# Half a group later: moving the attention of groups 4 to 7 behind the sums of a seven-product MLP2, and twelve row pairs instead of eight

## The chip, the cores and the metric

The kernel runs on one core of a Trainium2 chip. The metric is device time in microseconds (us) of that core; a result is the median of several executions. A program on one core has no second die to be compared with, so an execution counts as slow when it is over 1.5% above the fastest of the same kernel; such executions are left out of the ratios.

I number groups of two row tiles as the code does, 0 to 7. "Group 3's MLP2" in the change's short description is index 2. In group k, `c, d` are the two tiles of group k+1 and `e, f` those of group k+2. Lines of the changed kernel stand three lower than those of the kernel before in the part that matters (L667 became L664, L647 became L644, L698 became L695, L397 became L394).

## The reference

One transformer block in bfloat16, 2048 rows of 576, 32 heads of 18, MLP width 4608.

```
h  = x + attention(layernorm(x), wqkv) @ wo     # each row attends to rows s, s-2, ..., s-14
h2 = h + gelu(layernorm(h) @ w1 + b1) @ w2 + b2
```

The attention is a sliding dilated window of eight: a row's logits are eight dot products per head. The kernel does that on VectorE (multiply, then add up), and gives TensorE only the projections and the MLP.

## The kernel before

Row tiles go through the MLP in groups of two. TensorE does, for each group, MLP1 (324 matmuls), the projection `wo` of the next group's attention, and MLP2. VectorE does the attention of a later group meanwhile. Two pieces of it matter here, the query-key product with its maximum, and the value sum:

```python
def att_qk_one(j, i, home):            # 2.55 us multiply + 2.87 us of adds + 0.4 us
    att_qk_a(j); halo(j, 1); att_qk_b(j, i, 0, home)

def att_pv_a(j):                       # value sum, multiplication: 2.55 us
    ... in0=v_ring[j % 2] ..., in1=probs ..., op=ALU.mult

def att_pv_b(j):                       # its adds: 2.15 + 0.46 us, result in q_all[:, j]

def pv_sum(j):                         # cut: att_pv_a, halo, att_pv_b
    ...

def halo(j, t):                        # next tile's shifted keys or values, 144 KB
    nc.sync.dma_start(out=ring[j % 2][:, j // 2, :], in_=kv_dram[j, 0:P, t - 1, :])
```

`v_ring` holds one plane that each tile has to load anew. So the value sum of the second tile must wait for a load that can only start when the first tile's multiplication has read the plane.

A finished value sum is stored (`send_o`), then read back transposed (`read_o`) as `oT`, the weights of the projection.

MLP2 of groups 2 to 7 treats `rows` of the 18 row pairs with seven matmuls instead of eight (Strassen and Winograd's scheme): VectorE forms sums of activations (`h_sums`, tiles t=0 to 3) and of weights (`w2_sums`). The order on TensorE in group 5, whose projection comes first (group 4 has the same start and end; with 12 row pairs it has no `(7, hi)` and puts `"rest"` right behind `"6"` and `"d"`):

```python
steps = ["wo", "hc", (1, all_), "b", "h", "e", (7, lo), (2, all_), (6, all_), "6", ... (7, hi), "rest",
         "in", (5, all_), "f", "exp", (4, all_), "21", "22", "o1", "4", (3, all_), "12", "o0", "3"]
```

A number is one of the seven products on TensorE. `"b"`, `"d"`, `"f"` copy a bank of PSUM, the memory in which TensorE leaves its sums, on ScalarE. `"h"`, `"6"`, `"7"`, `"exp"`, `"4"`, `"3"` are hooks where other work is put into the engines' lists; `"rest"`, `"o1"`, `"o0"` are the output adds on VectorE that free PSUM banks.

The kernel before, in the loop over groups from 2 on (cut):

```python
ROWS = {2: 8, 3: 12, 4: 12, 5: 16, 6: NM, 7: NM}
m1[0] += [c_(pv_sum, d), c_(send_o, d), c_(read_o, d)]          # second value sum: in MLP1
m1[1] += [c_(att_qk_one, f, 1, home ^ 1), c_(att_max, (e, f))]  # second query-key product and maximum: in MLP1
x["exp"] += [c_(exps, e, f), c_(att_den, e, f)]
x["4"] += [c_(att_pv_a, e), c_(halo, e, 2)]                     # first value sum: in MLP2
x["3"] += [c_(att_pv_b, e), c_(send_o, e), c_(read_o, e)]
x["7"] += [c_(att_qk_one, GROUPS[k + 3][0], 0, home)]           # first query-key product: in MLP2
```

Of the kernel before, what the change touches and what calls it, by code (L numbers as in the profile page):

```python
# [12 lines left out]
F32 = mybir.dt.float32  # L13
# [4 lines left out]
def kernel(  # L18
# [16 lines left out]
    H = 32  # L35
    Dh = D // H
    W = 8
# [18 lines left out]
    GROUPS = [ATT_ORDER[i:i + 2] for i in range(0, NT, 2)]  # L56
# [14 lines left out]
    x_all = wpool.tile([P, NT, D], BF16, name="x_all")  # L71
# [11 lines left out]
    logits = wpool.tile([P, 2, W, H], F32, name="logits")  # L83
    probs = wpool.tile([P, 2, W, H], BF16, name="probs")
# [242 lines left out]

    side = {}

    def logit_of(js):  # L330
        home, i = side[js[0]]
        return (x_all[:, 13:16:2, 0:2 * W * H].bitcast(F32).rearrange("p i (w h) -> p i w h", w=W)
                if home else logits[:])[:, i:i + len(js)]

    def sides(js):
        i = side[js[0]][1]
        return slice(i, i + len(js))

    def halo(j, t):
        if j >= 2:  # L340
# [3 lines left out]
    def att_qk_a(j):  # L344
        nc.vector.tensor_tensor(out=prod[:], in0=k_ring[j % 2], in1=q_all[:, j, :].unsqueeze(1)  # L345
                                .to_broadcast([P, W, D]), op=ALU.mult)

    def att_qk_add(j, steps):
        for o, a, c in steps:
            n = (c - a if c < 9 else 9) * H  # L350
            nc.vector.tensor_tensor(out=prod[:, :, o * H:o * H + n], in0=prod[:, :, a * H:a * H + n],  # L351
                                    in1=prod[:, :, c * H:c * H + n], op=ALU.add)

    def att_qk_b(j, i, skip=0, home=0):
        side[j] = (home, i)
        out = logit_of([j])[:, 0]
        att_qk_add(j, ((0, 0, 9), (0, 0, 4), (0, 0, 2), (0, 0, 1))[skip:])
        nc.vector.tensor_tensor(out=out, in0=prod[:, :, 0:H], in1=prod[:, :, 8 * H:9 * H], op=ALU.add)
        if j // 2 + 1 < W:
            nc.vector.memset(out[0:1, j // 2 + 1:W, :], -1e9)  # L360
# [12 lines left out]
        halo(j, 1)  # L373
        att_qk_rest(j, i)

    def att_qk_one(j, i, home):
        att_qk_a(j)
        halo(j, 1)
        att_qk_b(j, i, 0, home)

    def att_exp(*js):
        lg = logit_of(js)
# [10 lines left out]
        nc.vector.tensor_tensor(out=probs[:, sl], in0=lg, in1=den[:, sl].unsqueeze(2).to_broadcast([P, n, W, H]), op=ALU.mult)  # L393

    def att_pv_a(j):
        a = probs[:, side.pop(j)[1]]
        nc.vector.tensor_tensor(out=prod[:].rearrange("p w (d h) -> p w d h", h=H),  # L397
                                in0=v_ring[j % 2].rearrange("p w (d h) -> p w d h", h=H),
                                in1=a.unsqueeze(2).to_broadcast([P, W, Dh, H]), op=ALU.mult)
# [139 lines left out]
    NM = FT // 2  # L539
# [139 lines left out]
    def c_(fn, *a):  # L679
        return lambda: fn(*a)  # L680
# [73 lines left out]
    with tc.manual_schedule(engines={ENG.PE, ENG.Activation, ENG.DVE, ENG.SP, ENG.Pool}):  # L754
# [222 lines left out]
        def wo_visit(*duos, fill=False):  # L977
            visit([wo_duo(j, tag) for j, tag in duos], (lambda: [ahead[0]() for _ in range(2)]) if fill else None)

        ROWS = {2: 8, 3: 12, 4: 12, 5: 16, 6: NM, 7: NM}  # L980
        p, q, r, s = "ABDC"

        gelu_table()
        for k, g in enumerate(GROUPS):
            c, d = GROUPS[k + 1] if k + 1 < len(GROUPS) else (None, None)
            e, f = GROUPS[k + 2] if k + 2 < len(GROUPS) else (None, None)
            m1, mid, ia, ib, late_wo = {0: []}, {}, {}, {}, None
            if k in (1, 2):
                m1[0].append(c_(finish_out, GROUPS[k - 1][1]))
            if k == 0:  # L990
                m1[0] += [c_(halos, 1), c_(load_w2, 4), c_(att_qk_a, d), c_(att_qk_rest, d, 1), c_(halo, d, 1)]
                mid[0] = {1: [c_(exps, d)]}
                m1[1] = [c_(pv_t, c), c_(pv_t, d), c_(att_qk_a, e), c_(halo, e, 1)]
                late_wo = wo_duo(c, "B")
                ia[0] = [c_(ln2_h, c), c_(ln2_act, c), c_(put_b2, c), c_(ln2_send, c), c_(att_qk_rest, e, 0)]
                ia[19] = [lambda d=d: wo_visit((d, "A"), fill=True), c_(ln2_h, d), c_(ln2_act, d), c_(put_b2, d), c_(att_qk_a, f),
                          c_(halos, 2), c_(halo, f, 1), c_(ln2_send, d), c_(ln2_ins, c, d), c_(att_qk_rest, f, 1), c_(exps, e, f)]
                ib[0] = [c_(finish_out, g[0]), c_(att_den, e, f), c_(pv_sum, e), c_(send_o, e)]
                ib[8] = [c_(read_o, e)]
            elif k == 1:  # L1000
                m1[0] += [c_(pv_sum, d), c_(send_o, d)]
                m1[1] = [c_(att_qk_a, e), c_(halo, e, 1), c_(read_o, d), c_(att_qk_b, e, 0), c_(halos, 7)]
                m1[3] = [c_(att_qk_a, f), c_(halo, f, 1), c_(att_qk_add, f, ((0, 0, 9), (0, 0, 4)))]
                ia[0] = [c_(wo_visit, (c, "B"), (d, "C")), c_(ln2_pair, c, d), c_(att_qk_b, f, 1, 2), c_(att_max, (e, f)),
                         c_(exps, e, f), c_(att_qk_one, GROUPS[4][0], 0, 1), c_(att_den, e, f)]
                ia[2] = [c_(pv_sum, e), c_(dma_tr_o, e), c_(reload_x, GROUPS[4])]
                ib[0] = [c_(finish_out, g[0])]
            if k < 2:
                mlp1(g, mlp1_plan(p, q, r, s, (s, r, p) if k else (r, s, p)), m1, mid, late_wo)
                mlp2_tile(g, 0, "D", ia)  # L1010
                mlp2_tile(g, 1, "C", ib)
                continue
            rows = ROWS[k]
            home = k % 2
            x = {n: [] for n in ("hc", "h", "6", "7", "in", "exp", "4", "3")}
            if k < 6:
                if k == 3:
                    m1[0] += [c_(w2_sums, 8, 12)]
                m1[0] += [c_(pv_sum, d), c_(send_o, d), c_(read_o, d)]
                m1[1] = [c_(accumulate_hs, *g)] if k == 2 else []  # L1020
                m1[1] += [c_(att_qk_one, f, 1, home ^ 1), c_(att_max, (e, f))]
                m1[3] = []
                if k == 2:
                    m1[3] += [c_(w2_sums, 0, 8)]
                early = {2: (), 4: (0, 2)}.get(k, (0,))
                m1[3] += [c_(h_sums, 0, min(rows, SR), early)]
                if k == 5:
                    x["h"] += [c_(h_sums, 0, SR, (2,)), c_(h_sums, 0, SR, (1, 3))]
                else:
                    x["h"] += [c_(h_sums, 0, rows, [t for t in range(4) if t not in early])]  # L1030
                if k == 5:
                    m1[1] += [c_(w2_sums, 12, 14)]
                    x["h"] += [c_(h_sums, SR, rows), c_(w2_sums, 14, 16)]
                x["exp"] += [c_(exps, e, f), c_(att_den, e, f)]
                x["4"] += [c_(att_pv_a, e), c_(halo, e, 2)]
                x["3"] += [c_(att_pv_b, e), c_(send_o, e), c_(read_o, e)]
            else:
                if k == 6:
                    m1[0] += [c_(pv_sum, d), c_(send_o, d), c_(read_o, d)]
                    ring1_free[0] = True  # L1040
                    m1[1] = [c_(w2_sums, 16, NM)]
                m1[3] = [c_(h_sums, 0, SR)]
                if k == 7:
                    mid[3] = {1: [c_(h_sums, SR, 16)]}
                    x["h"] += [c_(h_sums, 16, NM)]
            if k + 3 < len(GROUPS):
                x["7"] += [c_(att_qk_one, GROUPS[k + 3][0], 0, home)]
                x["in"] += [c_(reload_x, GROUPS[k + 3])]
            wo = None
            if c is not None:  # L1050
                if k == 6:
                    x["hc"] += [c_(ln2_h, c), c_(ln2_act, c)]
                    x["h"] += [c_(ln2_h, d), c_(ln2_more, d), c_(ln2_rstd, d), c_(h_sums, SR, NM), c_(ln2_send, c),
                               c_(ln2_bias, d), c_(add_b2, c), c_(add_b2, d)]
                    x["6"] += [c_(ln2_hn, d), c_(ln2_out, d)]
                else:
                    x["hc"] = [c_(ln2_h, c), c_(ln2_act, c)] + x["hc"]
                    x["h"] = [c_(ln2_h, d), c_(ln2_act, d), c_(put_b2, c), c_(put_b2, d)] + x["h"]
                    x["6"] += [c_(ln2_send, c)]
                    x["7"] = [c_(ln2_send, d)] + x["7"]  # L1060
                x["in"] = [c_(ln2_ins, c, d)] + x["in"]
                wo = lambda tags: wo_visit((c, tags[0]), (d, tags[1]))
            mlp1(g, mlp1_plan(p, q, r, s, (r, s, p)), m1, mid)
            if 4 <= k < 7:
                mlp2_fast(g, rows, (s, p, q, r), wo, x, True)
                p, q, r, s = q, r, p, s
            else:
                mlp2_fast(g, rows, (q, p, r, s), wo, x)
                p, q, r, s = r, s, p, q
# [30 lines left out]
```

## Time and profile before

| | kernel before |
|---|---|
| median | 364.16 us (363.96 to 365.28, 3 runs), span of the profiled run 362.6 us |
| TensorE busy | 357.3 us, 4895 matmuls |
| VectorE busy | 300.3 us |
| ScalarE busy | 228.9 us |
| TensorE clock granted | 1.0 in the profiled run |

TensorE is the bound: the chain of waits holds little else. Only work taken from it, or a new wait of it, changes the time.

These are two lines of the kernel before, from ScalarE's and from TensorE's timeline in group 4 (start, length, engine, line, operation):

```profile
240.56 0.39 ACT L738 COPY po<-po 128x288 f32<-128x288 f32 x1
238.99 3.41 PEld L667 LDWEIGHTS <-h_all 128*128 128x128 f16 x28
```

The copy is the seed `"b"` of group 4's MLP2. It ends at 240.95, and TensorE's 28 weight loads run through without a gap.

### The profile page before, as it was taken

To read this page: it belongs to the slowest core of one execution; us is meant where nothing else is said; L and a number is where in the kernel's file an instruction comes from. 1 tells how busy PE (TensorE), PEld (TensorE's weight loads), DVE (VectorE), ACT (ScalarE), POOL (GpSimd) and SP (SyncE) were. 2 spreads that over 40 slices of the span, in tenths; PEclk is the share of its full clock that TensorE was granted. 3 is DMA by queue.
4 is the path that set the end of the run, shared out by engine and by line. 5 is a ranking of instruction groups with operands and counts; after the bars stand their busy time and mean duration, and the time that the engine had idled before them with its cause. 6 is when DMAs were issued, how large, how long until landed. Compare 5 with 4: busy or idle time off the path is not lost.

```text
span 362.6 us, 11419 instructions
## 1 busy us (share of the span) xinstructions
PE 357.3 (99%) x4895; PEld 290.9 (80%) x4895; DVE 300.3 (83%) x422; ACT 228.9 (63%) x507; POOL 39.3 (11%) x47
## 2 busy tenths in 40 slices
PE   8999999999999999999999999999999999999996
PEld 4678877888778887887788778877887788778874
DVE  5899999999899999999999899998999498620441
ACT  4679846799536764568556864695469456705630
POOL 2241004000120030103100111020101100100000
PEclk9999999999999999999999999999999999999999
DMA  7979989964446833620552146304521352120001
GB/s 241 291 188 324 227 242 242 365 230 75 145 90 103 195 143 87 133 59 34 137 104 73 35 101 126 86 33 107 121 69 35 74 102 56 39 54 18 2 2 33
DMA packets 61908, 43.70 MB, mean 121 GB/s; under 512 B 31889, under 2 KB 60177, under 8 KB 61857
## 3 DMA queue, kind: packets, MB, share of 16 engines
q1 hardware_dynamic: 59968, 41.13, 41.7%
q0 software_dynamic: 1728, 1.77, 4.8%
q8 instruction: 38, 0.62, 0.7%
q14 instruction: 14, 0.11, 0.1%
q10 hardware_dynamic: 160, 0.07, 0.1%
HBM read 21.10 MB, written 12.42 MB: 92 GB/s over the span
## 4 chain that ended last, share of the span: by engine, by line
PE 96%; DMA 1%; SPq 1%; DVE 0%; issue 0%
PE pm L217 39%; PE po L667 27%; PE pq L217 14%; PE po L579 10%; PE pw L217 5%; DMA wq_sb<-in_A_wqkv_dram 1%; SPq L104 1%; PE xt_pt L182 1%; PE o_pt L182 0%; PE h_pt L182 0%; PE xt_pt L186 0%; DVE o_sb L698 0%; PE h_pt L186 0%; PE o_pt L186 0%; PE xt_pt L184 0%
## 5 line engine op out<-in xcount | busy, mean ns | idle before, releaser
L560 ACT ACTIVATE h_all<-pm,b_sb 128x256 f16<-128x256 f32 (+1 forms) x288 | 108.5, 497 | 74.8 <-PE pm L217 74.8
L217 PE MATMUL pm<-hnT,w_sb 64*128 64x256 bf16 x2304 | 143.0, 269 | 0.0
L217 PEld LDWEIGHTS <-w_sb 64*128 64x128 bf16 x2304 | 111.8, 94 | 15.0 <-issue 1.7
L667 PEld LDWEIGHTS <-h_all 128*128 128x128 f16 x528 | 50.9, 98 | 14.7 <-issue 1.8
L217 PE MATMUL pq<-wq_sb,xnT 64*128 64x288 bf16 x768 | 54.7, 283 | 1.0 <-DMA wq_sb<-in_A_wqkv_dram 1.0
L217 PEld LDWEIGHTS <-xnT 64*128 64x128 bf16 x864 | 42.1, 94 | 11.8 <-issue 1.0
L351 DVE TENSOR_TENSOR prod<-prod 128x2304 bf16<-128x2304 bf16 (+1 forms) x64 | 44.2, 691 | 2.1
L667 PE MATMUL po<-w2a_sb,h_all 128*128 128x288 bf16 (+1 forms) x302 | 41.5, 286 | 0.0
L397 DVE TENSOR_TENSOR prod<-kv_ring,probs 128x4608 bf16<-128x4608 bf16 x16 | 40.9, 2554 | 0.5 <-DMA kv_ring<-kv_dram 0.2
L345 DVE TENSOR_TENSOR prod<-kv_ring,q_all 128x4608 bf16<-128x4608 bf16 x16 | 40.8, 2549 | 0.2
L217 PE MATMUL pm<-hnT,w1h_sb 64*128 64x256 bf16 x288 | 39.2, 269 | 0.0
L403 DVE TENSOR_TENSOR prod<-prod 128x2304 bf16<-128x2304 bf16 (+1 forms) x32 | 33.8, 1056 | 1.0
L579 PEld LDWEIGHTS <-h_all 128*128 128x128 bf16 x288 | 27.8, 98 | 7.9 <-issue 0.9
L481 POOL TENSOR_TENSOR ln_rstd<-ln_var,mhalf 128x1 f32<-128x1 f32 x13 | 14.5, 1114 | 171.5 <-ACT ln_var L480 171.5
L579 PE MATMUL po<-w2a_sb,h_all 128*128 128x288 bf16 x224 | 28.5, 286 | 0.0
L667 PEld LDWEIGHTS <-kv_ring 128*128 128x128 f16 x240 | 23.5, 98 | 5.9
L667 PE MATMUL po<-w2b_sb,h_all 128*128 128x288 bf16 (+1 forms) x142 | 21.3, 286 | 0.0
L647 DVE TENSOR_TENSOR kv_ring<-h_all 128x1536 f16<-128x1536 f16 (+4 forms) x9 | 6.7, 745 | 16.0 <-ACT h_all L560 16.0
L217 PE MATMUL pw<-wo_sb,oT 64*128 64x288 bf16 x256 | 19.5, 283 | 0.0
L738 ACT COPY po<-po 128x288 f32<-128x288 f32 x18 | 6.9, 385 | 18.4 <-PE po L667 17.3
L162 POOL TENSOR_TENSOR ln_rstd<-ln_veps,mhalf 128x1 f32<-128x1 f32 (+2 forms) x14 | 13.1, 946 | 48.4 <-PE pq L217 31.2
L217 PEld LDWEIGHTS <-oT 64*128 64x128 bf16 x288 | 13.8, 94 | 4.2 <-issue 0.9
(117 smaller groups left out, 383.5 us busy)
## 6 DMA issues: line engine op xcount, KB each, us to landing
w_sb<-in_B_w_dram SPq DMA_DIRECT2D x6, 768.0 KB, 5.9
kv_ring<-kv_dram SPq DMA_DIRECT2D x28, 144.0 KB, 2.5
w2a_sb<-in_B_w_dram SPq DMA_DIRECT2D x4, 1008.0 KB, 6.4
kv_dram<-kv_ring SPq DMA_DIRECT2D x13, 288.0 KB, 4.0
out_dram<-o_sb SPq DMA_DIRECT2D x15, 144.0 KB, 2.8
td<-q_all SPq DMA_DIRECT2D x14, 144.0 KB, 2.0
td<-hn SPq DMA_DIRECT2D x14, 144.0 KB, 1.8
x_all<-in_A_x_dram SPq DMA_DIRECT2D x12, 144.0 KB, 2.7
```

Source lines behind the costliest of these rows:

```text
L162: nc.gpsimd.tensor_tensor(out=rstd[:], in0=veps[:], in1=mhalf[:].to_broadcast([P, n]), op=ALU.pow)
L217: last = nc.tensor.matmul(duo["g"][r ^ swap][i], lhsT=lhsT, rhs=rhs, start=(swap == 0 and i == 0 and kt == 0), stop=(swap == 1 and kt == K ...
L345: nc.vector.tensor_tensor(out=prod[:], in0=k_ring[j % 2], in1=q_all[:, j, :].unsqueeze(1) .to_broadcast([P, W, D]), op=ALU.mult)
L351: nc.vector.tensor_tensor(out=prod[:, :, o * H:o * H + n], in0=prod[:, :, a * H:a * H + n], in1=prod[:, :, c * H:c * H + n], op=ALU.add)
L397: nc.vector.tensor_tensor(out=prod[:].rearrange("p w (d h) -> p w d h", h=H), in0=v_ring[j % 2].rearrange("p w (d h) -> p w d h", h=H), in ...
L403: nc.vector.tensor_tensor(out=prod[:, 0:n, :], in0=prod[:, 0:n, :], in1=prod[:, n:2 * n, :], op=ALU.add)
L481: nc.gpsimd.tensor_tensor(out=rstd[:], in0=var[:], in1=mhalf[:], op=ALU.pow)
L560: pace[0] = nc.scalar.activation(out=hT(grp)[:, f, 0:N], in_=ps[:, r, i * N:(i + 1) * N], func=ACT.Gelu_apprx_tanh, bias=b1_sb[:, f:f + 1] ...
L579: nc.tensor.matmul(banks[half], lhsT=hT(grp)[:, f, i * P:(i + 1) * P], rhs=w2_rows(f)[:, half * HALF:(half + 1) * HALF], start=(f == 0), s ...
L647: nc.vector.tensor_tensor(out=s_slot(t, m0, m1), in0=a, in1=b, op=alu)
L667: nc.tensor.matmul(bank, lhsT=l, rhs=r, start=start, stop=stop, skip_group_check=True)
L738: nc.scalar.copy(out=bank[seed[step][1]], in_=bank[seed[step][0]])
```

## The change

Its intent is to take four more matmuls from group 2's MLP2. For this VectorE must have its sums ready sooner, so the attention of the later groups is put half a group later: the second query-key product and the maximum go into MLP2 behind the sums, and both value sums into the next MLP1, ahead of the projection that needs them. The core of the diff (cut; an extra buffer for logits falls away as well):

```diff
-        ROWS = {2: 8, 3: 12, 4: 12, 5: 16, 6: NM, 7: NM}
+        ROWS = {2: 12, 3: 12, 4: 12, 5: 16, 6: NM, 7: NM}
@@ group 1
-                         c_(exps, e, f), c_(att_qk_one, GROUPS[4][0], 0, 1), c_(att_den, e, f)]
+                         c_(exps, e, f), c_(w2_sums, 0, 8, (0, 1)), c_(w2_sums, 8, 12, (0, 1)), c_(att_den, e, f)]
@@ groups from 2 on
+            if 2 < k < 7:
+                m1[0] += [c_(pv_sum, c), c_(send_o, c), c_(pv_sum, d), c_(read_o, c), c_(send_o, d), c_(read_o, d)]
             if k < 6:
-                if k == 3:
-                    m1[0] += [c_(w2_sums, 8, 12)]
-                m1[0] += [c_(pv_sum, d), c_(send_o, d), c_(read_o, d)]
-                m1[1] += [c_(att_qk_one, f, 1, home ^ 1), c_(att_max, (e, f))]
+                m1[1], m1[3] = [c_(att_qk_one, e, 0)], []
                 if k == 2:
-                    m1[3] += [c_(w2_sums, 0, 8)]
+                    m1[0] += [c_(pv_sum, d), c_(send_o, d), c_(read_o, d)]
+                    m1[3] += [c_(w2_sums, 0, 8, (2, 3)), c_(w2_sums, 8, 12, (2, 3))]
...
-                x["exp"] += [c_(exps, e, f), c_(att_den, e, f)]
-                x["4"] += [c_(att_pv_a, e), c_(halo, e, 2)]
-                x["3"] += [c_(att_pv_b, e), c_(send_o, e), c_(read_o, e)]
+                x["7"] += [c_(att_qk_one, f, 1), c_(att_max, (e, f))]
+                x["exp"] += [c_(exps, e, f)]
+                x["4"] += [c_(att_den, e, f)]
@@ k + 3 < len(GROUPS)
-                x["7"] += [c_(att_qk_one, GROUPS[k + 3][0], 0, home)]
```

More of the change, by code (lines that the diff above doesn't have):

```diff
@@ L328, with sides @@
     side = {}
+    def sides(js):
+        return slice(side[js[0]], side[js[0]] + len(js))
     def logit_of(js):
-        home, i = side[js[0]]
-        return (x_all[:, 13:16:2, 0:2 * W * H].bitcast(F32).rearrange("p i (w h) -> p i w h", w=W)
-                if home else logits[:])[:, i:i + len(js)]
-    def sides(js):
-        i = side[js[0]][1]
-        return slice(i, i + len(js))
+        return logits[:, sides(js)]
     def halo(j, t):
@@ L352, in att_qk_add, with att_qk_b @@
                                     in1=prod[:, :, c * H:c * H + n], op=ALU.add)
-    def att_qk_b(j, i, skip=0, home=0):
-        side[j] = (home, i)
+    def att_qk_b(j, i, skip=0):
+        side[j] = i
         out = logit_of([j])[:, 0]
@@ L374, in att_qk, with att_qk_one @@
         att_qk_rest(j, i)
-    def att_qk_one(j, i, home):
+    def att_qk_one(j, i):
         att_qk_a(j)
         halo(j, 1)
-        att_qk_b(j, i, 0, home)
+        att_qk_b(j, i)
     def att_exp(*js):
@@ L395, in att_pv_a @@
     def att_pv_a(j):
-        a = probs[:, side.pop(j)[1]]
+        a = probs[:, side.pop(j)]
         nc.vector.tensor_tensor(out=prod[:].rearrange("p w (d h) -> p w d h", h=H),
@@ L1013 @@
             rows = ROWS[k]
-            home = k % 2
             x = {n: [] for n in ("hc", "h", "6", "7", "in", "exp", "4", "3")}
+            if 2 < k < 7:
+                m1[0] += [c_(pv_sum, c), c_(send_o, c), c_(pv_sum, d), c_(read_o, c), c_(send_o, d), c_(read_o, d)]
             if k < 6:
-                if k == 3:
-                    m1[0] += [c_(w2_sums, 8, 12)]
-                m1[0] += [c_(pv_sum, d), c_(send_o, d), c_(read_o, d)]
-                m1[1] = [c_(accumulate_hs, *g)] if k == 2 else []
-                m1[1] += [c_(att_qk_one, f, 1, home ^ 1), c_(att_max, (e, f))]
-                m1[3] = []
+                m1[1], m1[3] = [c_(att_qk_one, e, 0)], []
                 if k == 2:
-                    m1[3] += [c_(w2_sums, 0, 8)]
+                    m1[0] += [c_(pv_sum, d), c_(send_o, d), c_(read_o, d)]
+                    m1[1] = [c_(accumulate_hs, *g)] + m1[1]
+                    m1[3] += [c_(w2_sums, 0, 8, (2, 3)), c_(w2_sums, 8, 12, (2, 3))]
                 early = {2: (), 4: (0, 2)}.get(k, (0,))
@@ L1033 @@
                     x["h"] += [c_(h_sums, SR, rows), c_(w2_sums, 14, 16)]
-                x["exp"] += [c_(exps, e, f), c_(att_den, e, f)]
-                x["4"] += [c_(att_pv_a, e), c_(halo, e, 2)]
-                x["3"] += [c_(att_pv_b, e), c_(send_o, e), c_(read_o, e)]
+                x["7"] += [c_(att_qk_one, f, 1), c_(att_max, (e, f))]
+                x["exp"] += [c_(exps, e, f)]
+                x["4"] += [c_(att_den, e, f)]
             else:
                 if k == 6:
-                    m1[0] += [c_(pv_sum, d), c_(send_o, d), c_(read_o, d)]
                     ring1_free[0] = True
```

## The prediction

> I number groups as the code does, 0 to 7, c and d being the two tiles of the next group, e and f those of the one after it; "group 3's MLP2" of the title is index 2 (ROWS[2] goes from 8 to 12).
>
> **What bounds the kernel now.** I read the busy times, the chain that ended last, TensorE's own waits, and then the order in time of TensorE's weight loads, VectorE and the DMA queue.
>
> ```profile
> PE 357.3 (99%) x4895; PEld 290.9 (80%) x4895; DVE 300.3 (83%) x422; ACT 228.9 (63%) x507; POOL 39.3 (11%) x47
> PE 96%; DMA 1%; SPq 1%; DVE 0%; issue 0%
> ```
> TensorE has the whole span. In order of time the chain has nothing but TensorE from 9.78 us to 359.26; TensorE's list of waits holds 1.0 us for the first weights and 0.8 at the start. So time changes only by matmuls taken away and by waits that TensorE does not have today.
>
> ```profile
> 162.52 1.09 PE po L667 x8
> 163.60 2.31 PE pw L217 x36
> 165.92 15.79 PE po L667 x128
> ...
> 272.25 2.21 PE pw L217 x36
> 274.46 15.92 PE po L667 x128
> 290.38 17.79 PE pm L217 x324
> 308.17 2.21 PE pw L217 x36
> ```
> Start, length, piece. Group 2's MLP2 is the 8, the projection `pw`, the 128; group 5's MLP2 runs from 272.25 to 290.38; group 6's MLP1 is the 324, its projection starts at 308.17.
>
> VectorE is only 83% busy over the span, but nearly full in groups 3 to 5. The places where it hands work to TensorE:
>
> ```profile
> 254.97 0.75 DVE L698 TENSOR_TENSOR o_sb<-po,x_all 128x576 bf16<-128x576 f32 x1
> 255.64 2.14 DVE L403 TENSOR_TENSOR prod<-prod 128x2304 bf16<-128x2304 bf16 x2
> 257.82 0.46 DVE L404 TENSOR_TENSOR q_all<-prod 128x576 bf16<-128x576 bf16 x1
> 258.31 2.56 DVE L397 TENSOR_TENSOR prod<-kv_ring,probs 128x4608 bf16<-128x4608 bf16 x1
> ...
> 269.89 1.02 DVE L364 TENSOR_REDUCE peak<-logits 128x64 f32<-128x512 f32 x1
> ...
> 275.48 0.95 DVE L647 TENSOR_TENSOR h_all<-h_all 128x1536 f16<-128x1536 f16 x1
> ```
> ```profile
> 274.39 1.83 PEld L667 LDWEIGHTS <-h_all 128*128 128x128 f16 x16 [0.24 <-issue]
> 276.48 3.30 PEld L667 LDWEIGHTS <-h_all 128*128 128x128 f16 x28 [0.26 <-DVE h_all L647]
> ```
> This pair is the key. In group 5 the activation difference `h_all` (t=2 of the seven-product sums) ends on VectorE at 275.48 + 0.95 = 276.43; TensorE loads it at 276.48, and is free at about 276.4. Slack there is zero already: VectorE runs without a gap from 254.97 to 281.
>
> ```profile
> 301.44 0.34 SPq L193 DMA_DIRECT2D td<-q_all  x1
> 301.83 0.42 SPq L194 DMA_DIRECT2D td<-q_all  x1
> 304.85 1.21 SPq L433 DMA_TRANSPOSE oT<-td  x1
> ```
> The way from a finished value sum to the projection: store, wait, transpose. The transpose lands 2.8 us after issue (median of the DMA issues), so group 6's last value sum, done at 301.4, is in place at 307.65. The projection needs it at 308.17 + 0.61 = 308.8.
>
> **What the Trainium skill says.**
> - "TensorE: Matmul & The Clock Gate", section "Wait — 56ns, not 53.3ns?": warm matmuls start N / 2.4 GHz + 2.5 ns apart, 122.5 ns for N = 288. The trace agrees: 128 in 15.79 us is 123.4 ns. The 286 ns of the group row is latency and must not be used.
> - Same page, "Step-by-step: what each phase is for": TensorE is the only engine that reorders, and only its weight loads. Agreed: the load at 276.48 waits and nothing passes it. So an instruction put earlier in VectorE's list delays all behind it.
> - "ScalarE: Activation LUTs", section "What ACT_TABLE_LOAD costs": 1283 ns; the trace has 1.28 us. It matters for the later exponentials.
> - "DMA: Bandwidth & Descriptors", section "Latency and other measured facts": about 2 us of fixed cost per DMA, hence not shrinkable by size. The 144 KB halo loads have a median of 2.5 us here.
>
> **The change part by part.**
> *Twelve row pairs in group 2.* Each row pair takes 7 matmuls and not 8: four pairs more take away 4 matmuls (the built program confirms 4 fewer on TensorE). 4 x 0.123 = **0.49 us** less TensorE work. VectorE pays 4 x (0.95 - 0.68) = 1.1 us for larger sums in group 2. Does it fit? TensorE: 12 matmuls end at 164.0, projection to 166.3, 24 matmuls, and the product that needs the second sum starts at 169.27, as before (36 matmuls either way). VectorE: first `h` add at about 165.86, two of 0.67, two sums of 0.87 + 0.95: ready at 169.0. Fits by 0.2 us.
>
> *Weight sums moved.* The 8-to-12 ones leave group 3 (3.0 us of VectorE) for groups 1 and 2, where VectorE then waits anyway. No effect on TensorE.
>
> *Attention half a group later.* In groups 2 to 5 the second query-key product and the maximum now stand in MLP2 (behind the sums), and both value sums in the next MLP1. I walk VectorE through group 5, with the spacings of the trace. Before, from 254.97: output add 0.67, rest of the first value sum 2.67, second 5.27, query-key 6.31, maximum 1.66, weight sums 1.72, sum t=0 0.87, two `h` adds 1.34, t=2 0.95: 276.43. After: the output add can start when TensorE ends group 4's MLP2, 254.46 - 0.49, say 254.0 (the normalisation ends at about 253.95). Then 0.67, two whole value sums 2 x 5.27, 6.31, no maximum, 1.72, 0.87, 1.34, 0.95 = 22.4: **X = 276.4** plus w. TensorE, 0.49 earlier, wants it at 275.9. It waits 0.5 us, and the saving of group 2 is gone.
>
> w: the second value sum needs the halo load that starts when the first one's multiplication ends; only the adds (2.65 us) lie between, against a landing of 2.5 us median, 3.4 us in the one tight case before (108.03 issued, multiplication at 111.52 after a 0.17 wait). w is 0 to 0.7, I take **0.3**.
>
> *Group 6.* From X: TensorE starts MLP1 at X + 13.95 (290.38 - 276.43) and needs the last transposed value sum at X + 13.95 + 17.79 + 0.61 = X + 32.35. VectorE after X: remaining sums 5.0, query-key 6.3 and maximum 1.65 (X + 12.95), the two PSUM releases 0.67 + 0.73, normalisation 2.27, output add 0.67: X + 17.3. They are released in time: `rest` is done at X + 13.65, TensorE wants that bank at X + 13.95. Two value sums of 5.25 and w (0.3) end at X + 28.1; before it was X + 24.9. Store to landed transpose took 5.1 to 7.4 us in groups 2 to 6; 5.9 taken: X + 34.0. TensorE waits **1.65 us** (0.5 to 3).
>
> *Groups 3 and 4.* Same walk: last value sums end at about 193.5 and 229.2 (193.1 and 227.6 before); landed at about 199.3 and 235.2; needed at 201.2 and 236.1. Fits. In group 5 they end at 265.5; a late landing there hides in front of X.
>
> *Exponentials.* They now follow the maximum: end 0.7 us later, table load 1.28 us. First gelu of the next MLP1 comes over 2 us later in each group. No wait.
>
> Sum: -0.49 + 0.5 + 0.3 + 1.65 = about +1.9.
>
> **The rivals.**
> 1. *The saving stands*: all sums arrive in time, 364.16 - 0.49 = 363.7. For it: the change was surely made for that, and my walk misses by few tenths in group 5. Against it: the zero slack at 276.48, and a later last value sum in group 6.
> 2. *Only group 5 bites*: the group 6 transposes take the shortest 5.1 us and w is 0; then +0.0 to +0.5: 364.2 to 364.7. One of five transfers was that short.
> 3. *More waits*: w near 0.7 in every group, so that groups 3 and 4 are late by their projection too, and group 6 waits 3 us: 367 to 368. Against it: their slack of 1 to 2 us.
> 4. *ScalarE or PSUM become the bound*: `rest` behind the maximum frees a bank just 0.3 us ahead of group 6's MLP1. An extra wait of some tenths, no more.
>
> **Range and chances.** Centre 364.16 + 1.9 = **366.0**. Low 363.7 is rival 1 whole, high 367.6 both waits at their upper ends. 2% is 7.3 us: no sum of these waits gets there, and no gain above 0.49 exists. Faster 0.01, same 0.97, slower 0.02.
>
> **What the profile afterwards would show.** Right: TensorE with 4 matmuls fewer and still no wait in groups 2 to 4; weight loads from `h_all` in group 5 waiting about 0.5 to 1 us for VectorE; weight loads from `oT` in group 6's projection waiting 0.5 to 3 us for a DMA; VectorE with small waits for `kv_ring` loads between value sums. Wrong: group 6's projection starting without a wait (transposes faster than 5 us, or VectorE ahead of my walk), or a wait in groups 2 to 4, or ScalarE's first gelu delayed by the table load. The point most likely to fail is the size of group 6's wait: it is the small difference of two long sums.

## The result, and the profile after

The changed kernel takes **366.21 us** (365.62 to 366.30, 6 runs) against 364.19 us (363.96 to 365.28, 6 runs) of the kernel before in the same rounds. The ratio is 1.0048, 95% interval 1.0035 to 1.0062: half a per cent slower, inside the 2% that counts as the same. A ratio is the mean time of one kernel's fast runs over that of the other's of the same rounds, so it is not quite the ratio of the medians quoted. Both profiled runs had a granted clock of 1.0; their spans are 362.6 and 364.5 us.

Busy times and the engines' shares of the chain of waits, from the page of the changed kernel:

```profile
PE 357.1 (98%) x4891; PEld 290.9 (80%) x4891; DVE 301.6 (83%) x422; ACT 229.4 (63%) x507; POOL 36.4 (10%) x47
PE 80%; DVE 9%; DMA 5%; SPq 2%; issue 1%; ACT 1%; DVEq 0%
```

Four matmuls are gone, yet TensorE's share of the chain has dropped from 96% to 80%: VectorE and DMAs have entered it. TensorE's list of waits (what waited, for what: us in total, times, longest) has two entries that were not there:

```profile
PE po L664 <- DVE h_all L644: 1.0, 1, 1.0
PE pw L217 <- DMA oT<-td: 0.6, 1, 0.6
```

The chain in order of time (start, length, piece; "..." stands for 0.05 us of "issue") shows both in their place:

```profile
276.62 0.88 DVE h_all L644
...
277.54 13.89 PE po L664 x112
291.44 16.10 PE pm L217 x293
307.54 2.88 DMA oT<-td
...
310.46 1.77 PE pw L217 x26
```

Group 5's MLP2 starts its 112 matmuls when VectorE has finished `h_all`, and group 6's projection its last 26 when a transposed value sum has landed. Before, both rows began behind other TensorE rows.

VectorE's timeline of the changed kernel gives the way to the first of them (in square brackets: idle before, and what ended it):

```profile
254.54 0.76 DVE L695 TENSOR_TENSOR o_sb<-po,x_all 128x576 bf16<-128x576 f32 x1 [0.23 <-PE po L664]
255.21 2.55 DVE L394 TENSOR_TENSOR prod<-kv_ring,probs 128x4608 bf16<-128x4608 bf16 x1
...
261.25 2.56 DVE L394 TENSOR_TENSOR prod<-kv_ring,probs 128x4608 bf16<-128x4608 bf16 x1 [0.81 <-DMA kv_ring<-kv_dram]
...
276.54 0.95 DVE L644 TENSOR_TENSOR h_all<-h_all 128x1536 f16<-128x1536 f16 x1
```

From output add to `h_all` there is no idle time but the 0.81 us between the two value sums, where the load of the value plane is late. `h_all` ends at 277.49, TensorE would have gone on at about 276.56.

SyncE's queue shows the way to the second wait:

```profile
305.48 0.34 SPq L193 DMA_DIRECT2D td<-q_all  x1
305.87 0.42 SPq L194 DMA_DIRECT2D td<-q_all  x1
307.54 1.21 SPq L430 DMA_TRANSPOSE oT<-td  x1
```

The last value sum ended at 305.46, its store was issued at once, its transpose 2.1 us later, and it landed at 310.42 (the chain's 307.54 + 2.88).

For every kernel below I read one table from the trace: the time from one MLP1's first matmul to the next one's, in TensorE's order of time. Where nothing differs, two profiles agree in it to about 0.03 us, so it shows tenths that a median over the whole kernel hides (the start of group 2's MLP1 alone scatters from 143.94 to 144.93 us over the fast profiles, for reasons that lie ahead of group 1: that group takes 37.74 or 37.75 us in all of them but the last kernel's, where it takes 37.86).

| us per group | 2 | 3 | 4 | 5 | 6 |
|---|---|---|---|---|---|
| before | 36.97 | 36.49 | 36.27 | 35.92 | 35.54 |
| changed | 36.50 | 36.49 | 36.52 | 36.93 | 36.34 |
| difference | -0.47 | 0 | +0.25 | +1.01 | +0.80 |

Group 7 takes 33.39 or 33.40 us in all. The sum of the differences is +1.59 us; the profiled spans differ by 1.9, of which 0.27 is the later start of group 2's MLP1, and the medians by 2.0.

### The profile page after: what moved, and what is told of

It is laid out like the page before. It is cut to its first block, busy times and chain, and to the rows that moved or that the text cites. A ratio compares the mean times of both kernels' runs of the same rounds, so it can differ in the third digit from the quotient of the medians.

```text
span 364.5 us, 11408 instructions
## 1 busy us (share of the span) xinstructions
PE 357.1 (98%) x4891; PEld 290.9 (80%) x4891; DVE 301.6 (83%) x422; ACT 229.4 (63%) x507; POOL 36.4 (10%) x47
## 4 chain that ended last, share of the span: by engine, by line
PE 80%; DVE 9%; DMA 5%; SPq 2%; issue 1%; ACT 1%; DVEq 0%
PE pm L217 29%; PE po L664 23%; PE pq L217 14%; PE po L576 10%; PE pw L217 4%; DVE prod L394 3%; DMA kv_ring<-kv_dram 2%; DVE prod L348 2%; DMA wq_sb<-in_A_wqkv_dram 1%; DVE prod L342 1%; DMA x_all<-in_A_x_dram 1%; DVE prod L400 1%; SPq L493 1%; SPq L104 1%; DMA oT<-td 1%
## 5 line engine op out<-in xcount | busy, mean ns | idle before, releaser
L664 PEld LDWEIGHTS <-h_all 128*128 128x128 f16 x512 | 49.4, 98 | 15.5 <-issue 2.1
L217 PEld LDWEIGHTS <-xnT 64*128 64x128 bf16 x864 | 43.0, 94 | 11.2 <-issue 1.0
L664 PE MATMUL po<-w2a_sb,h_all 128*128 128x288 bf16 (+1 forms) x282 | 39.2, 286 | 1.1 <-DVE h_all L644 1.0
L664 PEld LDWEIGHTS <-kv_ring 128*128 128x128 f16 x252 | 24.6, 98 | 6.3
L478 POOL TENSOR_TENSOR ln_rstd<-ln_var,mhalf 128x1 f32<-128x1 f32 x13 | 11.7, 901 | 172.9 <-ACT ln_var L477 172.9
L644 DVE TENSOR_TENSOR kv_ring<-h_all 128x1536 f16<-128x1536 f16 (+3 forms) x9 | 6.8, 760 | 14.7 <-ACT h_all L557 14.7
L458 DVE TENSOR_TENSOR h<-pw,x_all 128x576 f32<-128x576 f32 x16 | 11.5, 752 | 8.2 <-PE pw L217 8.2
L162 POOL TENSOR_TENSOR ln_rstd<-ln_veps,mhalf 128x1 f32<-128x1 f32 (+2 forms) x14 | 13.0, 939 | 48.6 <-DVE ln_veps L156 30.1
```

The lines of the kernel that those rows point to most:

```text
L162: nc.gpsimd.tensor_tensor(out=rstd[:], in0=veps[:], in1=mhalf[:].to_broadcast([P, n]), op=ALU.pow)
L217: last = nc.tensor.matmul(duo["g"][r ^ swap][i], lhsT=lhsT, rhs=rhs, start=(swap == 0 and i == 0 and kt == 0), stop=(swap == 1 and kt == K ...
L458: nc.vector.tensor_tensor(out=h[:].rearrange("p (g c) -> p g c", g=2), in0=pw[:, :, 0:HALF], in1=x_of(j).rearrange("p (g c) -> p g c", g=2 ...
L478: nc.gpsimd.tensor_tensor(out=rstd[:], in0=var[:], in1=mhalf[:], op=ALU.pow)
L664: nc.tensor.matmul(bank, lhsT=l, rhs=r, start=start, stop=stop, skip_group_check=True)
```

## The experiments

Each result was correct. My theory: the four matmuls are saved in full, and the attention's new place costs more than they bring, at three hand-overs: the sums of group 5 (VectorE has no slack, and a halo load between two value sums adds to it), the transposed value sums of group 6, and something in group 4. The rivals: the larger sums of twelve row pairs cost the time by themselves; or the new PSUM and exponential order does.

**The same kernel again.** First, does the result repeat? The changed kernel, nothing edited.

> The changed kernel itself, on the same chip as the runs sent with it. My theory, after seven runs: stage by stage (from one MLP1's first matmul to the next one's) group 2 is 0.47 us shorter than before, group 5 is 0.4 to 1.1 us longer and group 6 0.7 to 0.8 us longer, where group 5's part above 0.4 is the landing of the halo load and so differs from run to run: about 365.5 to 366.3 us. Rival (the first trace was one bad draw): below 365.

366.28 us (365.87 to 366.63) against 364.48, ratio 1.0044 (1.0021 to 1.0067). By group 36.51, 36.48, 36.53, 37.08, 36.29; waits 1.1 us for `h_all` and 0.6 for `oT`. All three losses repeat, group 4's too.

**The row pairs alone.** The kernel before with twelve pairs in group 2 and nothing moved but the weight sums they need.

```diff
-        ROWS = {2: 8, 3: 12, ...
+        ROWS = {2: 12, 3: 12, ...
-                if k == 3:
-                    m1[0] += [c_(w2_sums, 8, 12)]
-                    m1[3] += [c_(w2_sums, 0, 8)]
+                    m1[3] += [c_(w2_sums, 0, 8), c_(w2_sums, 8, 12)]
```

> The kernel before with twelve row pairs in group 2 and nothing else: attention stays where it was, the weight sums 8 to 12 stand beside those of 0 to 8. My theory: the row pairs save 0.47 us of TensorE, but VectorE is full up to group 2's MLP2, so 3.0 us of weight sums push its sums behind the product that needs them; TensorE waits about 2.3 us in group 2, time about 366.0 us. Rival (the row pairs are free and the attention move is all that costs): 363.7 us, no wait of TensorE.

368.04 us (366.36 to 368.42) against 364.62, ratio 1.0088 (1.0051 to 1.0126). One of the 11 runs of the kernel before took 368.24 us at a granted clock of 0.995; it is within 1.5% and counts as fast, so it widens the intervals. Five of the six runs had a mean granted clock of 0.995; the profiled one, 366.36 us, had 1.0, so the median holds more than the wait. The groups of the profiled run are 39.19, 36.49, 36.27, 35.93, 35.57. One wait is new:

```profile
PE po L667 <- DVE kv_ring L647: 2.5, 1, 2.5
```

So the matmuls can't be had without moving VectorE's work: its sums then come 2.5 us late, in group 2 and nowhere else. That is what the change's attention half is for.

**The attention alone.** The changed kernel with eight pairs.

```diff
-        ROWS = {2: 12, ...
+        ROWS = {2: 8, ...
-                    m1[3] += [c_(w2_sums, 0, 8, (2, 3)), c_(w2_sums, 8, 12, (2, 3))]
+                    m1[3] += [c_(w2_sums, 0, 8, (2, 3))]
+                if k == 3:
+                    m1[3] += [c_(w2_sums, 8, 12, (2, 3))]
```

> The changed kernel with eight row pairs in group 2 again (weight sums 8 to 12, the in-place half, go to group 3 where VectorE waits). My theory: the waits of groups 4, 5 and 6 come from the attention order, not from the larger sums; they stay (about 0.25, 1.0 and 0.7 us) and TensorE has its 0.47 us back: about 366.7 us. Rival (the larger sums of group 2 make VectorE late): waits gone, 364.2 us.

365.36 us (364.82 to 366.06) against 364.62, ratio 1.0011 (0.9981 to 1.0042). By group 36.98, 36.49, 36.27, 36.33, 36.29. Groups 5 and 6 lose 0.41 and 0.75 us with eight pairs as well, so their loss belongs to the attention's place. It is smaller in group 5 than I expected, and group 4 loses nothing: here VectorE waited only 0.21 us for the load in group 5 and not at all in group 4. This is one profile, so it does not show whether the eight pairs or chance made the load land sooner.

**Is the slack in group 5 really zero?** The kernel before, with one activation sum of group 5 (t=0) done twice, 0.87 us more of VectorE and the same values.

```diff
-                m1[3] += [c_(h_sums, 0, min(rows, SR), early)]
+                m1[3] += [c_(h_sums, 0, min(rows, SR), early)] * (2 if k == 5 else 1)
```

> The kernel before with one sum of group 5's MLP1 done twice (128x1536, 0.87 us of VectorE, result the same). My theory: the hand-over at 276.4 us has no slack, so the whole 0.87 us appears: 365.0 us, TensorE waiting for VectorE's h_all about 0.9 us in group 5. Rival (VectorE is idle for 17% of the span and takes it up): 364.2 us.

The profile's groups are 36.97, 36.49, 36.27, 36.90, 35.54: +0.98 in group 5, nothing elsewhere, with this wait of TensorE:

```profile
PE po L667 <- DVE h_all L647: 0.9, 1, 0.9
```

The median was 365.64 us (365.02 to 367.47), ratio 1.0026 (0.9992 to 1.0061). What delays VectorE ahead of this sum delays TensorE by as much, already in the kernel before.

**First value sums back in MLP2.** The changed kernel, with the first tile's value sum where it was, so that no two value sums stand together.

```diff
-                m1[0] += [c_(pv_sum, c), c_(send_o, c), c_(pv_sum, d), c_(read_o, c), c_(send_o, d), c_(read_o, d)]
+                m1[0] += [c_(pv_sum, d), c_(send_o, d), c_(read_o, d)]
-                x["4"] += [c_(att_den, e, f)]
+                x["4"] += [c_(att_den, e, f), c_(att_pv_a, e), c_(halo, e, 2)]
+                x["3"] += [c_(att_pv_b, e), c_(send_o, e), c_(read_o, e)]
```

> The changed kernel with the first value sum's multiplication ahead of the output add, as before the change, the second value sum alone in the MLP1: 0.67 + 2.65 us then lie between the two multiplications, and the halo load has time. My theory: VectorE no longer waits for the halo load (0.59 and 0.81 us in groups 4 and 5), group 4's wait goes, group 5's falls from 1.0 to about 0.2, group 6's stays near 0.7: about 365.1 us. Rival (the load is not what makes VectorE late, the order of the query-key product is): 366.0 to 366.2 us.

365.18 us (364.39 to 370.0; the 370.0 is slow) against 364.62, ratio 1.0005 (0.9971 to 1.0038). The profiled run was the slow one, so I ran it again:

> The kernel of e3_value_split once more, since its profile fell in a slow run. That profile showed a new wait of 1.1 us in group 6's MLP1 on the output add of group 5, which stands behind the value sum's multiplication (2.6 us) and so frees its PSUM banks late. My theory: the wait is of the kernel and not of the slow run: group 5 as before the change, group 6 about 1.2 us longer than before, no wait for oT: about 364.9 us. Rival (the wait belongs to the slow run): group 6 0.7 longer, waiting for oT.

364.93 us (364.71 to 365.45) against 364.48, ratio 1.0008 (0.9985 to 1.0031). By group 36.50, 36.48, 36.28, 35.84, 36.82. The losses of groups 4 and 5 are gone, and the wait for `oT` too, but group 6 now loses 1.28 us, 1.10 of it in a wait that neither kernel has:

```profile
295.92 0.28 PE L217 MATMUL pm<-hnT,w_sb 64*128 64x256 bf16 x2 [1.10 <-DVE o_sb L695]
```

This is in group 6's MLP1. The output add of group 5 (`o_sb`), which frees a PSUM bank, now stands in VectorE's list behind the maximum, the denominator and the first value sum's multiplication. My theory had not foreseen this wait: the work has to be somewhere in a full VectorE list, and each place blocks someone else.

**Fill the gap between the value sums.** The changed kernel, with 0.9 us of weight sums put between group 5's two value sums, where VectorE idled 0.81 us.

```diff
+            if k == 5:
+                m1[0] += [c_(pv_sum, c), c_(send_o, c), c_(w2_sums, 12, 14, (0, 1)), c_(pv_sum, d), ...]
-                    m1[1] += [c_(w2_sums, 12, 14)]
+                    m1[1] += [c_(w2_sums, 12, 14, (2, 3))]
```

> The changed kernel with two weight sums of group 5 (0.85 us in all) moved between the two value sums, into the gap where VectorE waits 0.81 us for the halo load; same work, same order otherwise. My theory: the gap is filled, group 5's wait of TensorE falls from 1.0 to 0.2 us, groups 4 and 6 stay: about 365.4 us. Rival (group 5's wait is set by the order of attention alone): 366.2 us.

364.48 us (364.22 to 365.33, 5 runs) against 364.48, ratio 1.0005 (0.9993 to 1.0017). The profile, of its slowest run, has groups of 36.50, 36.48, 36.28, 36.64, 36.28: VectorE waited 0.65 us for the load all the same, because this time it landed 4.1 us after issue. So the groups of one profile and the median don't agree well here, and I draw only this from it: the load's landing is no constant.

**Move weight sums to where VectorE idles.** In group 2 the changed kernel's VectorE idles 4.7 us ahead of its first `h` add. Half the weight sums of row pairs 12 to 15 (t=0 and 1) move there from group 5.

```diff
-                    m1[3] += [..., c_(w2_sums, 8, 12, (2, 3))]
+                    m1[3] += [..., c_(w2_sums, 8, 12, (2, 3)), c_(w2_sums, 12, 14, (0, 1)), c_(w2_sums, 14, 16, (0, 1))]
-                    m1[1] += [c_(w2_sums, 12, 14)]
-                    x["h"] += [c_(h_sums, SR, rows), c_(w2_sums, 14, 16)]
+                    m1[1] += [c_(w2_sums, 12, 14, (2, 3))]
+                    x["h"] += [c_(h_sums, SR, rows), c_(w2_sums, 14, 16, (2, 3))]
```

> The changed kernel with four weight sums of rows 12 to 16 (1.7 us) taken out of group 5 and done in group 2, where VectorE waits 4.7 us for the projection. My theory: group 5's VectorE is 0.85 us earlier ahead of the hand-over and 0.85 us shorter behind it, so group 5's wait falls to about 0.15 and group 6's to about 0; group 4's 0.25 stays: about 364.6 us. Rival (group 6's wait is the transposing DMA's own time and does not follow VectorE): group 6 keeps 0.6, 365.3 us.

363.97 us (363.45 to 365.15) against 364.48, ratio 0.9997 (0.9983 to 1.0011). By group 36.50, 36.48, 36.27, 35.79, 35.55: every loss is gone, the saving of group 2 stays, and group 5 is even 0.13 us shorter than in the kernel before, which had no slack there. A second sample:

> The kernel of e5_sums_early once more: its profile had no wait of TensorE after the first weights, and its stages from group 2 on were 0.6 us shorter than those of the kernel before, but two of six times were 365 us. My theory: halo loads that land late eat its margin of some tenths in some executions; 363.7 to 364.0 us against 364.3 for the kernel before. Rival (it is no faster than the kernel before): ratio at 1.000 or above.

364.2 us (363.40 to 365.56), ratio 0.999 (0.996 to 1.002). By group 36.50, 36.48, 36.57, 36.45, 35.54. Groups 4 and 5 lose again, +0.30 and +0.53. The same line of VectorE's timeline, of the first profile and then of the second, tells why:

```profile
260.18 2.56 DVE L394 TENSOR_TENSOR prod<-kv_ring,probs 128x4608 bf16<-128x4608 bf16 x1 [0.61 <-DMA kv_ring<-kv_dram]
```

```profile
261.03 2.56 DVE L394 TENSOR_TENSOR prod<-kv_ring,probs 128x4608 bf16<-128x4608 bf16 x1 [1.32 <-DMA kv_ring<-kv_dram]
```

The same program waited 0.61 us in one execution and 1.32 in the other. The 0.9 us of weight sums taken from in front of `h_all` covered the first and not the second. Group 6's wait fell away in both, although nothing in its own stretch was changed: of the sums that VectorE has to do behind `h_all` in group 5 some 0.9 us stand in group 2 now, so the value sums of group 6 come earlier.

**Both of these, and a mixture.** First the value-sum split with the early weight sums; then the early weight sums with the split in groups 2 to 4 only.

> Both repairs: first value sum's multiplication ahead of the output add, and four weight sums of rows 12 to 16 in group 2. My theory: no wait of TensorE left after the first weights, and the 0.47 us of the row pairs show: 363.7 us, faster than both kernels. Rival (some other wait takes the place of these): 364.2 us or more.

364.21 us (363.65 to 364.76, 5 runs), ratio 0.9993 (0.9982 to 1.0005). By group 36.50, 36.49, 36.27, 35.78, 35.84: the PSUM wait is gone, but group 6 still loses 0.30, of which 0.2 is a wait for `oT`. The rest needs no other wait: in the changed kernel, its repeat, the eight pairs and the filled gap the profile counts 0.6 us of this wait where the group loses 0.74 to 0.80.

> e5_sums_early with the first value sum's multiplication ahead of the output add in groups 2 to 4 only: the halo load then has over 3 us in groups 3 to 5, and group 5's output add still frees its banks early. My theory: no halo wait of VectorE ahead of group 5, no wait of TensorE, 363.6 us with fewer late runs than e5. Rival (an output add or a transpose comes late instead, as in e3 and e6): 364.0 or more and a wait of TensorE in groups 3 to 6.

363.80 us (363.34 to 364.60) against 364.48, ratio 0.998 (0.9956 to 1.0004): the lowest median of all, with an interval that just includes 1. Its profile fell on the slowest of its runs, with groups 36.50, 36.49, 36.27, 36.61, 35.59. There the load was issued at 256.36 (SyncE's queue) and the value sum that needs it waited 1.81 us, until 261.37 (VectorE's timeline):

```profile
256.36 0.33 SPq L339 DMA_DIRECT2D kv_ring<-kv_dram  x1
```

```profile
261.37 2.56 DVE L394 TENSOR_TENSOR prod<-kv_ring,probs 128x4608 bf16<-128x4608 bf16 x1 [1.81 <-DMA kv_ring<-kv_dram]
```

Issued 1.4 us earlier than in the changed kernel (257.79), it landed no earlier: some 4.9 us after issue, while the sum in the changed kernel started at 261.25. This is what needed an explanation.

**What holds up the load?** Ahead of it, GpSimd issues two accumulating loads (`x_all<-h`, L505), at 252.96 to 254.13 us in the seven profiles in which VectorE waits in group 5. In these seven, group 5's second value sum started 6.9 to 7.5 us after that issue, whether the halo load itself was issued 2.9 or 5.0 us before the sum. This picks out the cases with a wait. In the split with the early weight sums the same two issues stood almost as in the mixture (accumulating loads at 254.16, against 253.91 there), and the sum started without a wait:

```profile
256.51 0.33 SPq L339 DMA_DIRECT2D kv_ring<-kv_dram  x1
```

```profile
259.83 2.56 DVE L394 TENSOR_TENSOR prod<-kv_ring,probs 128x4608 bf16<-128x4608 bf16 x1
```

So that load landed within 3.3 us, and in the kernel before, 1.25 us behind the accumulating loads, in 2.6. Their nearness alone does not make it late. In the stretch from 252 to 263 us the two kinds of queue in the first profile with early weight sums stand so (packets, MB, share of the time of 16 DMA engines):

```profile
q1 hardware_dynamic: 1074, 0.91, 30.9%
q0 software_dynamic: 288, 0.30, 25.2%
```

The accumulating loads are GpSimd's, the software queue: a quarter of the bytes, nearly half of the busy time (they also turn float32 `h` into bfloat16, so what the accumulation itself costs is not shown). So the last kernel, the one with the early weight sums, put them behind the transposes of the next value sums.

```diff
+        read[0] = nc.sync.dma_start_transpose(out=new_oT(j)[:], ...).ins      # accumulating loads wait for this
-            if c not in (GROUPS[2][0], GROUPS[-1][0]):
+            if c not in (GROUPS[2][0], GROUPS[4][0], GROUPS[5][0], GROUPS[-1][0]):
                 accumulate_hs(c, d)
+                if k in (4, 5):
+                    m1[1] = [c_(accumulate_hs, *g)] + m1[1]
```

> The kernel of e5_sums_early with one thing more: the two accumulating loads (x_all<-h) that GpSimd issues at the end of groups 3 and 4, at about 217 and 253 to 254 us, are put behind the transposes of the value sums of the next MLP1, so some 12 us later. Theory A (the halo load between the two value sums lands late because it shares the DMA engines with these accumulating loads: in seven runs the second value sum of group 5 started 6.9 to 7.5 us after they were issued, whether the load itself was issued 2.8 or 4.9 us before that start): the load lands about 2.1 to 2.5 us after its issue, VectorE's wait ahead of the second value sum in groups 4 and 5 is 0 (it was 0.61 in group 5 of e5_sums_early, 0.64 and 1.32 in its repeat), no TensorE wait for h_all, groups 4 and 5 at about 35.8 and 35.55 us, median about 363.7 us. Theory B (the lateness is of the queue on SyncE or of the load itself): landing stays above 3 us and VectorE waits 0.3 to 1.3 us as in e5_sums_early and its repeat, 363.9 to 364.2 us. Either could fail if the accumulating loads now collide with the transposes of the value sums: then a wait for oT shows.

401.04 us (399.84 to 401.91) against 364.52, ratio 1.1 (1.0975 to 1.1026). Both theories missed by 37 us, for a reason outside them. By group 45.99, 36.49, 49.10, 49.70, 35.54. The chain in order of time (cut), TensorE's row in group 5's MLP1 and GpSimd's row:

```profile
289.95 2.78 DMA oT<-td
...
293.32 0.50 POOL x_all L505
...
293.87 14.11 PE pm L217 x159
```

```profile
293.87 4.45 PE L217 MATMUL pm<-hnT,w_sb 64*128 64x256 bf16 x40 [11.37 <-POOLq L227]
```

```profile
293.29 1.78 POOL L505 DMA_DIRECT2D x_all<-h  x2 [26.58 <-DVE prod L348]
```

L227 is the marker: an empty instruction on GpSimd that tells TensorE that half a bank's matmuls have ended. It stands in GpSimd's list behind the accumulating loads. These now waited for a transpose that landed at 292.73, the marker waited behind them, and TensorE 11.4 us for the marker; likewise in groups 2 and 4 (7.5 and 11.3 us), as the edit holds for group 2's accumulating loads as well. This agrees with what the Trainium skill states in "PSUM — Partial Sum Buffer", section "Engine vs sequencer instructions": the queues of ScalarE, VectorE and GpSimd are strict FIFO. The three waits are 30.1 us. Most of the rest is that the granted clock was 0.50 to 0.61 just after each: the next 40 matmuls took 3.8 to 4.5 us, where they take 2.35 elsewhere. I had looked for a collision of transfers and not at who stands behind in the queue.

On the question itself the run says little. With no accumulating load near, group 4's second value sum did not wait and group 5's did, 0.40 us, its load landing at most 3.05 us after issue (279.57 to 282.62). So the loads of GpSimd are not the whole of it, and the 4.9 us was not seen; but TensorE, and with it the whole stretch, ran at other times here. What makes the halo load late stays open.

## Why the prediction was right

Predicted 366.0 us, range 363.7 to 367.6; measured 366.21. The class, the sign and the mechanism of groups 2, 5 and 6 held; in group 4 there is a wait that the prediction had excluded, and had named as a sign of being wrong. By its steps:

- **Four matmuls less in group 2**: predicted -0.49 us, measured -0.47, and the second sum was ready in time, as the walk through VectorE said. Row pairs alone (+2.22 us in group 2) show that this is so only with the attention moved.
- **Group 5's hand-over**: predicted to start with zero slack. The run with 0.87 us more of VectorE cost 0.98 us there. The walk from output add to `h_all` was 22.4 us and 0.3 of waiting; measured 22.95 (254.54 to 277.49), with 0.81 of waiting. So `w` was sized too small, at 0.3 for 0.81 (0.96 in the repeat), both above the 0 to 0.7 that it allowed, and the work in between 0.25 too large. The group's loss was predicted as 0.5 + 0.3 = 0.8, and is 1.01.
- **Group 6's projection**: predicted wait 1.65 us, measured 0.63, for which the group is 0.80 longer. The last value sum ended at 305.46, 27.97 us after `h_all` (predicted 28.1), and TensorE wanted it at 310.46 - 0.63 = 309.83, 32.34 us after (predicted 32.35). The term that failed is "5.9 taken" from store to landed transpose: it took 4.9 to 5.0. The text itself named this size as the point most likely to fail.
- **Group 4**: "fits" was wrong. It loses 0.25 us, by a path that I did not walk. VectorE waited 0.59 us for the halo load there too, so its `h` adds and with them ScalarE's normalisation come later, and the seed copy stands behind that normalisation in ScalarE's list. The lines that answer to the two shown for the kernel before:

```profile
240.67 0.39 ACT L735 COPY po<-po 128x288 f32<-128x288 f32 x1
```

```profile
238.91 1.94 PEld L664 LDWEIGHTS <-h_all 128*128 128x128 f16 x16
241.11 1.32 PEld L664 LDWEIGHTS <-h_all 128*128 128x128 f16 x11 [0.27 <-issue]
```

  The copy ends at 241.06 and the loads go on at 241.11, 0.27 us late. The profile names no releaser there, so that it is the copy rests on the times, and on this: the three profiles with a wait of 0.59 us or more for the load in group 4 lose 0.25 to 0.30 there, those with 0.34 or less lose nothing.
- **Exponentials, gelu**: predicted without a wait, and there is none.

The sum was -0.49 + 0.5 + 0.3 + 1.65 = +1.96; the groups measured -0.47 + 0.25 + 1.01 + 0.80 = +1.59. An overrated wait in group 6 (by 0.85) and two underrated ones in groups 4 and 5 (by 0.46) partly cancel, and some 0.4 us of the 2.0 between the medians is not in these groups at all (0.27 is the later start). So the closeness of 366.0 to 366.21 is in part luck. A slip in the range changes nothing: with both waits at their upper ends (0.5 + 0.7 and 3) the sum is 367.9, not 367.6.

Of the rivals, the first ("the saving stands") is what the early weight sums nearly give: 363.97 and 364.2 us against its 363.7. The second ("only group 5 bites") falls with the wait for `oT`. The third came in part, as group 4's wait, but not where I put it. The fourth, PSUM as the bound, is not in the changed kernel, but is what the value-sum split ran into.

No version beat the kernel before beyond doubt. The mixture, 363.80 us, is the best candidate, at 0.2% with an interval up to 1.0004.

## What to carry to other kernels

Removing work from the bounding engine pays only if the engine that feeds it has slack at each hand-over; before moving work of a nearly full engine, list each hand-over in order of time with its slack, and follow what its lateness does to third engines (here ScalarE's copy behind its normalisation). Two steps that share one buffer, put side by side, expose the reload between them: a few microseconds that differ from run to run, so leave room for the worst of them and not for the median. And before an instruction is made to wait longer, look at everything behind it in the same engine's list.

## What the Trainium skill lacked or had wrong

- "DMA: Bandwidth & Descriptors" gives about 2 us of fixed cost per DMA, and for the access to HBM alone 0.2 us on average and 2 us at high load, but no spread of a whole load: the same 144 KB halo load took 2.1 to 4.9 us to land here, its median over the kernel 2.5 us before and 3.1 after.
- The same page says that accumulating loads are issued from GpSimd, but not what they cost. Here those that GpSimd issued had a median of 4.0 us to landing, against 2.5 to 3.1 for plain loads of the same 144 KB, and took 25.2% of the DMA engines' time for 0.30 MB where the hardware queue took 30.9% for 0.91 MB.
- "SBUF — State Buffer", section "SBUF: two separate sides", describes loads issued by GpSimd whose descriptors wait while VectorE runs an operation in a two-port mode, and says that a load issued by ScalarE or SyncE does not suffer from it. The late halo loads here (up to 4.9 us) are SyncE's, and no profile shows VectorE's mode, so this does not explain them; I found no page that does.
- "PSUM — Partial Sum Buffer" has the strict order of GpSimd's queue, but no page has a warning that empty synchronising instructions put on GpSimd are held up by a waiting DMA issue ahead of them: 7.5, 11.3 and 11.4 us of TensorE in three groups here.
- What was drawn on in the prediction held: 123.4 ns per matmul of 288 columns against the stated 122.5, and 1.28 us for a table load.
